# A slot's edges before the sums, the reciprocal behind the fold, and one stop at which nothing is evicted

## The chip, the cores and the metric

The kernel runs on one core of a Trainium2 chip. The metric is the device time of one execution in microseconds (us); lower is better. The engines are TensorE (PE in the profile, with its weight loads as PEld), VectorE (DVE), ScalarE (ACT), GpSimd (POOL) and SyncE (SP), which here only starts DMAs.

## The reference

Attention in which each query keeps its 32 highest scores, and then four matrix products on the result. All of it is float32.

```python
B, H, S, D = 8, 8, 576, 64
scores = (1.0 / np.sqrt(D)) * np.matmul(q, k.transpose(0, 1, 3, 2))
kth = np.partition(scores, -32, axis=-1)[..., -32:-31]
scores = np.where(scores >= kth, scores, -1000000000.0)
scores = scores - np.max(scores, axis=-1, keepdims=True)
attn = np.exp(scores)
attn = attn / (np.sum(attn, axis=-1, keepdims=True) + 1e-09)
x = np.matmul(attn, v).transpose(0, 2, 1, 3).reshape(B * S, H * D)   # 4608 x 512
return (((x @ w1) * (x @ w2)) @ w3) @ w_out                          # 512 -> 1024 -> 1024 -> 512
```

## The kernel before

The attention is cut into 144 **slots**, 18 for each of the 8 batches. A slot is 128 queries of two heads (the last 64 queries of two head pairs share a slot, the one with `t == 4`). The matrix products of a batch, 576 TensorE instructions, are handed out during the 18 slots of the next batch, 32 a slot. Those of the last batch come behind the last slot. In the first 15 slots or so the weights are still fetched and decoded, by `warm()`.

The loop of line 514 is a software pipeline. In its turn `p` it computes the scores of slot `p+1`, finds the 32 highest of slot `p`, masks and exponentiates slot `p-1` (`j`) and multiplies slot `p-2` (`m`) with the values. Each engine works through its own queue in the order in which the loop issues, since `InOrder` (line 39) keeps the program order; semaphores are added where data demand it. The names of a turn, in the order of the queues:

- **fold** (VectorE, `top32_steps`, line 234): four tensor_tensor instructions that write `w` out of the scores `s`. Three rounds of MAX8 and MATCH_REPLACE8 follow, and a last MAX8 over 576 columns, which completes `top`. Last comes `xt`, the scaled output (`store_x`).
- **edge** and `over` (GpSimd, `edges_of`, line 257): tiny instructions on `top`. ScalarE's first step of masking (`mask`, called **relu** here: `pab<-s,edge`) needs the edge. GpSimd's two subtractions `pab<-s,pab` follow, the first of them behind the next slot's fold, by a dependency written out by hand.
- **sums** (GpSimd) and **reciprocal** (VectorE), both in `invert`, line 295: 1e-9 is added to the two sums that ScalarE's second exponential has just completed, and they are inverted. TensorE spreads them over the partitions (`ro<-ident,sums`).
- **chunks' copy** (ScalarE, `take_turned`, line 313): the transposed weights `tp` go from PSUM to `pts`; TensorE's product with the values (`ro<-pts,vt`) waits for it.

The order at the top of a turn, lines 521 to 527:

```python
if 0 <= m < n_slots:
    invert(pabs[m][1])
folded = next(finder, None)
warm()
if 0 <= j < n_slots:
    edges[j] = edges_of(j)
    pabs[j] = new_weights()
```

The matrix products fill in at four stops of a turn, `fill(SHARE[0])` to `fill(SHARE[3])`, with 8, 3, 11 and 10 matmuls. What must be done when a PSUM tile is complete is **put off**: `moe_steps` appends it to `put_off`, and the next `fill` runs all of that list (`evict`, line 473) ahead of its matmuls. Put off are `asb` (ScalarE copies the product with w1), `whole` with its two followers `g` (VectorE multiplies it with the product with w2, ScalarE and GpSimd split the result into a high and a low part), `osb` (ScalarE copies the output) and `split_x` (`xf`, two ScalarE and two GpSimd instructions). Behind `fill(SHARE[1])` come TensorE's transposes `tp`, and ScalarE's chunks' copy. PSUM has three tiles for these products.

Of the kernel before, what the change touches and what calls it, by code (L numbers as in the profile page):

```python
# [34 lines left out]
SHARE = 8, 3, 11, 10  # L35
# [22 lines left out]
def attn_moe(ctx: ExitStack, tc: tile.TileContext, q, k, v, w1, w2, w3, w_out, out, flag, general):  # L58
# [123 lines left out]
    def new_ro():  # L182

        return ps_v.tile([128, 512], F32, tag="v", name="ro")

    def last_scores(pairs, t, ro):

        sc = ro[:, 384:]
        if t == 4:
            for a in range(2):  # L190
                qt, kt, _ = pairs[a]
                for i in range(2):
                    pe.matmul(
                        sc[:, a * 64 : a * 64 + 64], qt[:, MAIN:], kt[:, MAIN + i * 64 : MAIN + i * 64 + 64],
                        start=(i == 0), stop=(i == 1),
                    )
        else:
            qt, kt, _ = pairs[0]
            pe.matmul(sc, qt[:, t * 128 : (t + 1) * 128], kt[:, MAIN:], start=True, stop=True)
        return sc  # L200
# [19 lines left out]
    def new_s():  # L220
        return att_p.tile([128, 2, S], F32, tag="s", name="s", bufs=3)
# [5 lines left out]
    def take_last(s, sc):  # L227
        act.copy(flat(s)[:, MAIN : MAIN + 128], sc)

    def take_scores(s, st):  # L230
        to = s[:, :, :MAIN]
        act.copy(bass.AP(tensor=to.tensor, offset=to.offset, ap=[to.ap[0], [S + 64, 2], [1, MAIN]]), st)

    def top32_steps(s, slot):

        w = att_p.tile([128, 2, S], F32, tag="w", name="w", bufs=1)
        top = tops[slot % len(tops)]
        one, two, three = slice(0, NG), slice(NG, 2 * NG), slice(2 * NG, S)
        dve.tensor_tensor(w[:, :, three], s[:, :, one], s[:, :, two], op=ALU.max)
        dve.tensor_tensor(w[:, :, two], s[:, :, one], s[:, :, two], op=ALU.min)
        dve.tensor_tensor(w[:, :, one], w[:, :, three], s[:, :, three], op=ALU.max)
        yield dve.tensor_tensor(w[:, :, three], w[:, :, three], s[:, :, three], op=ALU.min)
        for i in range(4):
            cut = slice(i * 8, (i + 1) * 8)
            for a in range(2):  # L250
                dve.max(top[:, a, cut], w[:, a, one] if i < 3 else w[:, a, :])
            if i < 3:
                for a in range(2):
                    dve.match_replace(w[:, a, one], top[:, a, cut], w[:, a, one], NEG)
                yield

    def edges_of(slot):
        top = tops[slot % len(tops)]
        edge = small.tile([128, 2, 2], F32, tag="edge", name="edge")
        pool.tensor_tensor(edge, top[:, :, 0:32:31], coef, op=ALU.mult)  # L260
        pool.tensor_tensor(over[:, 2 * slot : 2 * slot + 2], top[:, :, 31], top[:, :, 23], op=ALU.subtract)
        return edge
# [15 lines left out]
    def new_weights():  # L278
        return att_p.tile([128, 2, S], F32, tag="pab", name="pab"), small.tile([128, 2], F32, tag="sums", name="sums")

    def mask(s, edge, pab, a, after=None):

        act.activation(pab[:, a, :], s[:, a, :], AF.Relu, bias=edge[:, a, 1:2], scale=-STEEP)
        ins = pool.tensor_tensor(pab[:, a, :], s[:, a, :], pab[:, a, :], op=ALU.subtract)
        if after is not None:
            tc.add_manual_dep(
                ins.ins, after.ins.name, mybir.DependencyInfo(mybir.DependencyClass.Sync, mybir.DependencyReason.DATA),
                reason="the fold of the next slot goes before the masking",
            )
# [5 lines left out]
    def invert(sums):  # L295
        pool.tensor_scalar(sums, sums, 1e-9, None, op0=ALU.add)
        dve.reciprocal(sums, sums)

    def turn(pab):

        tp = ps_a.tile([128, 2, 512], F32, tag="a", name="tp")
        for a in range(2):
            for c in range(4):
                n, o = (a * 4 + c) * 64, a * (S + 64) + c * 128
                for i, rows in enumerate(HEADS):
                    pe.transpose(tp[:, i, n : n + 64], flat(pab)[rows, o : o + 128], ident[rows, rows])
        return tp

    def turn_last(pab, ro):

        pe.transpose(ro[:, :128], flat(pab)[:, MAIN : MAIN + 128], ident)

    def take_turned(tp):
        pts = att_p.tile([128, 2, 512], F32, tag="pts", name="pts", bufs=1)
        act.copy(pts, tp)
        return pts

    def take_last_turned(ro):
        pr = att_p.tile([128, 128], F32, tag="pr", name="pr")
        act.copy(pr, ro[:, :128])  # L320
        return pr
# [146 lines left out]
    kv, ss, edges, pabs, xts = {}, {}, {}, {}, {}  # L468
# [4 lines left out]
    def evict():  # L473
        while put_off:
            put_off.pop(0)()

    def fill(n):
        evict()
        while queue and n:
            if next(queue[0], "end") == "end":  # L480
                queue.pop(0)
            else:
                n -= 1

    def pairs_of(i):
        return [kv[u] for u in slots[i][0]]

    def fetch_pair(u):
        if u < B * NHP:
            kv[u] = load_pair(u // NHP, u % NHP)  # L490
# [9 lines left out]
    def warm():  # L500

        if p < 0:
            return
        if fetched:
            z, step = fetched.pop(0)
            going.append(step(z))
        going[:] = [unit for unit in going if next(unit, "end") != "end"]
        prefetch(5)
# [4 lines left out]
    n_slots = len(slots)  # L513
    for p in range(-1, n_slots + 3):
        i, j, m = p + 1, p - 1, p - 2
        if i < n_slots and slots[i][1] == 3:
            fetch_pair(slots[i][0][0] + 2)
        while starting:
            queue.append(moe_steps(*starting.pop(0), put_off.append))
        finder = top32_steps(ss[p], p) if 0 <= p < n_slots else iter(())  # L520
        if 0 <= m < n_slots:
            invert(pabs[m][1])
        folded = next(finder, None)
        warm()
        if 0 <= j < n_slots:
            edges[j] = edges_of(j)
            pabs[j] = new_weights()
            for a in range(2):
                mask(ss[j], edges[j], pabs[j][0], a, folded if a == 0 else None)
        fill(SHARE[0])  # L530
        if 0 <= m < n_slots or i < n_slots:
            ro = new_ro()
        if 0 <= m < n_slots:
            turn_last(pabs[m][0], ro)
        if i < n_slots:
            sc = last_scores(pairs_of(i), slots[i][1], ro)
        if 0 <= m < n_slots:
            pr = take_last_turned(ro)
        if i < n_slots:
            ss[i] = new_s()  # L540
            take_last(ss[i], sc)
        fill(SHARE[1])
        next(finder, None)
        if 0 <= m < n_slots:
            tp = turn(pabs[m][0])
        if i < n_slots:
            st = scores(pairs_of(i), slots[i][1])
        if 0 <= m < n_slots:
            pts = take_turned(tp)
        if i < n_slots:  # L550
            take_scores(ss[i], st)
        warm()
        if 0 <= j < n_slots:
            exps(edges[j], *pabs[j], 0)
        if 0 <= m < n_slots:
            us, t = slots[m]
            for u in us:
                if u not in xts:
                    xts[u] = new_xt()
            ov, rb = values([kv[u][2] for u in us], t, pts, pr, pabs[m][1], ro)  # L560
            rec = take_rb(rb)
        if ready and (m + 1) % NS:
            put_off.append(lambda x=ready[0]: split_x(x[2], x[1], 0, 1))
            starting.append(ready.pop(0))
        fill(SHARE[2])
        next(finder, None)
        warm()
        if 0 <= j < n_slots:
            exps(edges[j], *pabs[j], 1)
        next(finder, None)  # L570
        warm()
        fill(SHARE[3])
        for _ in finder:
            pass
        if 0 <= m < n_slots:
            store_x([xts[u] for u in us], t, ov, rec)
            del ss[m], pabs[m], edges[m]
            if (m + 1) % NS == 0:
                ready.append((m // NS, [xts[m // NS * NHP + hp] for hp in range(NHP)], ([], [])))
                put_off.append(lambda x=ready[0]: split_x(x[2], x[1], 0, 0))  # L580
        warm()
# [69 lines left out]
```

## Time and profile before

| | |
|---|---|
| median of 3 runs | 1362.36 us (1360.36 to 1364.18) |
| profiled execution: its time, its span | 1362.26 us, 1360.5 us |
| PE, DVE, ACT, POOL busy | 1249.0, 1159.1, 980.7, 792.1 us |
| PEld busy | 1019.4 us |
| first and last relu start | 20.4, 1253.3 us |

The profiled execution is within 0.1 us of the median, and its span is 1.8 us shorter than its time. The span has three parts: the first 207 us, in which weights are prepared and VectorE hardly rests; from there to 1253 us slot after slot beside the matrix products; and the products that are left, to the end. The middle part repeats itself every 18 slots to within 0.03 us.

### The profile page before, as it was taken

To read this page: it belongs to the slowest core of one execution; us is meant where nothing else is said; L and a number is where in the kernel's file an instruction comes from. 1 tells how busy PE (TensorE), PEld (TensorE's weight loads), DVE (VectorE), ACT (ScalarE), POOL (GpSimd) and SP (SyncE) were. 2 spreads that over 40 slices of the span, in tenths; PEclk is the share of its full clock that TensorE was granted. 3 is DMA by queue.
4 is the path that set the end of the run, shared out by engine and by line. 5 is a ranking of instruction groups with operands and counts; after the bars stand their busy time and mean duration, and the time that the engine had idled before them with its cause. 6 is when DMAs were issued, how large, how long until landed. Compare 5 with 4: busy or idle time off the path is not lost.

```text
span 1360.5 us, 33364 instructions
## 1 busy us (share of the span) xinstructions
PE 1249.0 (92%) x12049; PEld 1019.4 (75%) x12049; DVE 1159.1 (85%) x4060; ACT 980.7 (72%) x2169; POOL 792.1 (58%) x1033
## 2 busy tenths in 40 slices
PE   3788846999999999999999999999999999999996
PEld 1444433788888888888888888888888888888996
DVE  7999999898989899999989898989999998987000
ACT  5777787777777777777777777777777777777221
POOL 3677696665656556565566565655656556656220
PEclk9998968999999999999999999999999999999998
DMA  6443431002020201011010202020101101000000
GB/s 221 117 132 104 137 93 31 21 17 64 13 68 12 68 13 52 29 44 36 25 44 17 64 12 68 13 68 12 49 32 45 36 14 56 16 15 2 19 18 21
DMA packets 34754, 65.15 MB, mean 48 GB/s; under 512 B 3860, under 2 KB 12052, under 8 KB 34580
## 3 DMA queue, kind: packets, MB, share of 16 engines
q1 hardware_dynamic: 34580, 62.93, 14.7%
q8 instruction: 97, 1.59, 0.5%
q14 instruction: 77, 0.63, 0.1%
HBM read 53.48 MB, written 9.44 MB: 46 GB/s over the span
## 4 chain that ended last, share of the span: by engine, by line
PE 54%; DVE 25%; ACT 8%; POOL 6%; issue 3%; DMA 1%; SPq 0%; DVEq 0%; POOLq 0%; ACTq 0%
PE ab L49 16%; PE eo L49 14%; PE ro L49 14%; DVE w L49 11%; DVE top L49 9%; PE st L49 5%; PE tp L49 3%; POOL edge L49 3%; ACT pab L49 3%; ACT pts L49 2%; DVE whole L49 2%; PE pf L49 2%; POOL g L49 2%; DVE y L49 1%; DVE z L49 1%
## 5 line engine op out<-in xcount | busy, mean ns | idle before, releaser
L49 POOL TENSOR_TENSOR pab<-s,pab 128x576 f32<-128x576 f32 x288 | 400.9, 1414 | 196.9 <-DVE w L49 101.2
L49 DVE MAX8 top<-w 128x8 f32<-128x192 f32 (+1 forms) x1152 | 466.7, 446 | 0.0
L49 PE MATMUL ab<-xf,wh 128*128 128x288 f32 x2048 | 432.8, 299 | 0.5 <-POOL xf L49 0.5
L49 PEld LDWEIGHTS ab<-xf,wh 128*128 128x128 f32 x2048 | 333.5, 188 | 10.5 <-issue 9.9
L49 ACT ACTIVATE pab<-s,edge 128x576 f32<-128x576 f32 x288 | 208.0, 769 | 159.5 <-POOL edge L49 159.5
L49 PE MATMUL ab<-xf,wl 128*128 128x288 f32 x1024 | 310.5, 303 | 0.0
L49 DVE MATCH_REPLACE8 w<-top,w 128x192 f32<-128x192 f32 x864 | 289.2, 342 | 0.0
L49 ACT ACTIVATE pab<-pab,edge 128x576 f32<-128x576 f32 x288 | 227.6, 790 | 0.8 <-POOL pab L49 0.7
L49 PE MATMUL eo<-g,wf 128*128 128x288 f32 x1536 | 228.1, 300 | 0.0
L49 PEld LDWEIGHTS eo<-g,wf 128*128 128x128 f32 x1536 | 208.6, 188 | 7.0 <-issue 7.0
L49 PEld LDWEIGHTS ab<-xf,wl 128*128 128x128 f32 x1024 | 192.2, 188 | 3.3 <-issue 2.4
L49 PE MATMUL ro<-pts,vt 128*64 128x128 f32 (+1 forms) x2560 | 163.4, 272 | 26.8 <-ACT pts L49 26.7
L49 POOL TENSOR_TENSOR g<-whole,g 128x288 fp32r<-128x288 f32 x128 | 103.1, 806 | 117.3 <-ACT g L49 117.3
L49 ACT COPY pts<-tp 128x1024 f32<-128x1024 f32 x144 | 146.0, 1014 | 32.7 <-PE tp L49 32.6
L49 PEld LDWEIGHTS ro<-pts,vt 128*64 128x64 f32 x2560 | 131.1, 140 | 48.9 <-ACT pts L49 42.3
L49 PE MATMUL st<-kt,qt 64*128 64x512 f32 (+1 forms) x640 | 165.7, 653 | 0.0
L49 DVE TENSOR_TENSOR w<-s 128x384 f32<-128x384 f32 x288 | 157.6, 587 | 8.7 <-ACT s L49 8.7
L49 DVE TENSOR_TENSOR w<-w,s 128x384 f32<-128x384 f32 x288 | 160.3, 557 | 4.9
L49 ACT COPY s<-st 128x1024 f32<-128x1024 f32 x144 | 147.0, 1021 | 4.0 <-PE st L49 3.9
L49 DVE TENSOR_TENSOR whole<-ab,asb 128x288 f32<-128x288 f32 x128 | 57.9, 452 | 99.1 <-PE ab L49 99.1
L49 PEld LDWEIGHTS ro<-ident,sums 128*64 128x64 f32 x640 | 31.0, 137 | 125.5 <-issue 50.8
L49 POOL TENSOR_SCALAR sums<-sums 128x2 f32<-128x2 f32 x144 | 30.7, 213 | 135.0 <-ACT pab L49 126.6
(52 smaller groups left out, 1572.6 us busy)
## 6 DMA issues: line engine op xcount, KB each, us to landing
z<-in_w SPq DMA_DIRECT2D x64, 256.0 KB, 2.6
vt<-in_v SPq DMA_DIRECT2D x32, 352.0 KB, 3.9
qt<-in_q SPq DMA_DIRECT2D x32, 320.0 KB, 3.0
kt<-in_k SPq DMA_DIRECT2D x32, 320.0 KB, 3.5
out_t<-osb SPq DMA_DIRECT2D x64, 144.0 KB, 1.8
z<-in_wo SPq DMA_DIRECT2D x16, 256.0 KB, 5.0
flag<-missed SPq DMA_DIRECT2D x1, 0.0 KB
seen<-flag SPq DMA_DIRECT2D x1, 0.0 KB
```

The costliest lines, as they stand in the source:

```text
L49: ins = fn(*args, **kw)
```

## The change

`edges_of` now stands ahead of `invert`, and `invert` behind the fold's issue and `warm()`. `fill` gets an argument `late`, with which it doesn't evict, and `fill(SHARE[1])` is called with it: what is put off in the first fill of a turn, or was going to be run at the second, is run at the third.

```diff
-    def fill(n):
-        evict()
+    def fill(n, late=False):
+        if not late:
+            evict()
         while queue and n:
...
         finder = top32_steps(ss[p], p) if 0 <= p < n_slots else iter(())
-        if 0 <= m < n_slots:
-            invert(pabs[m][1])
         folded = next(finder, None)
         warm()
         if 0 <= j < n_slots:
             edges[j] = edges_of(j)
+        if 0 <= m < n_slots:
+            invert(pabs[m][1])
+        if 0 <= j < n_slots:
             pabs[j] = new_weights()
...
-        fill(SHARE[1])
+        fill(SHARE[1], late=True)
         next(finder, None)
```

VectorE's queue in a turn whose first fill completes a product with w2 (`top_97` is one of three buffers that take turns), before:

```order
L49 TENSOR_TENSOR xt<-ro,rec 128x128
L49 RECIPROCAL sums<-sums 128x2
L49 TENSOR_TENSOR w<-s 128x2x192 x2
L49 TENSOR_TENSOR w<-w,s 128x2x192 x2
L49 TENSOR_TENSOR whole<-ab,asb 128x288
L49 MAX top_97<-w 128x8 x2
L49 MATCH_REPLACE w<-top_97,w 128x192 x2
```

and now:

```order
L49 TENSOR_TENSOR xt<-ro,rec 128x128
L49 TENSOR_TENSOR w<-s 128x2x192 x2
L49 TENSOR_TENSOR w<-w,s 128x2x192 x2
L49 RECIPROCAL sums<-sums 128x2
L49 MAX top_97<-w 128x8 x2
L49 MATCH_REPLACE w<-top_97,w 128x192 x2
L49 TENSOR_TENSOR whole<-ab,asb 128x288
```

The reciprocal moved from ahead of the fold to behind it, and `whole` from ahead of the first round to behind it.

GpSimd's queue in the same turn, before:

```order
L49 TENSOR_TENSOR g<-whole,g 128x288
L49 TENSOR_SCALAR sums<-sums 128x2
L49 TENSOR_TENSOR edge<-top_97,coef 128x4
L49 TENSOR_TENSOR over<-top_97 128x2
L49 TENSOR_TENSOR pab<-s,pab 128x576 x2
```

and now:

```order
L49 TENSOR_TENSOR g<-whole,g 128x288
L49 TENSOR_TENSOR edge<-top_97,coef 128x4
L49 TENSOR_TENSOR over<-top_97 128x2
L49 TENSOR_SCALAR sums<-sums 128x2
L49 TENSOR_TENSOR pab<-s,pab 128x576 x2
```

The edge and `over` passed the sums, and nothing else on GpSimd changed its place here.

ScalarE's queue in the same turn, before:

```order
L49 ACTIVATE pab<-s,edge 128x576 x2
L49 COPY asb<-ab 128x288
L49 COPY pr<-ro 128x128
L49 COPY s<-ro 128x128
L49 CAST g<-whole 128x288
L49 COPY pts<-tp 128x1024
L49 COPY s<-st 128x2x512
L49 ACTIVATE pab,sums<-pab,edge 128x576
L49 COPY rec<-ro 128x128
L49 ACTIVATE pab,sums<-pab,edge 128x576
```

and now:

```order
L49 ACTIVATE pab<-s,edge 128x576 x2
L49 COPY asb<-ab 128x288
L49 COPY pr<-ro 128x128
L49 COPY s<-ro 128x128
L49 COPY pts<-tp 128x1024
L49 COPY s<-st 128x2x512
L49 ACTIVATE pab,sums<-pab,edge 128x576
L49 COPY rec<-ro 128x128
L49 CAST g<-whole 128x288
L49 ACTIVATE pab,sums<-pab,edge 128x576
```

The cast `g` moved from ahead of the chunks' copy `pts` to behind `rec`. Over nine slots, which is half a batch, this move meets `whole` and `g` twice, `asb` twice, and `xf` and `osb` once each. TensorE's queue and SyncE's have the same order as before.

## Rows read from the trace of the kernel before

**Rows 1.** Stretches: us, busy PE, PEld, DVE, ACT, POOL (instructions); clock, DMA share, GB/s

```profile
0.00:207.00 207.00, 141.83 (x899) 74.89 (x899) 190.91 (x589) 151.44 (x369) 140.94 (x194) 0.90 0.44 132
555.17:702.90 147.73, 144.88 (x1492) 122.46 (x1492) 135.35 (x487) 113.62 (x246) 88.52 (x114) 1.00 0.12 37
```

**Rows 2.** Waits: engine, line <- releaser: us in total, times, longest us

```profile
ACT pab L49 <- POOL edge L49: 159.5, 142, 3.0
...
PE ro L49 <- ACT pts L49: 26.7, 68, 1.3
```

**Rows 3.** Timeline, TensorE, four slots: start, us, what [idle before <-releaser]

```profile
592.59 1.09 PE L49 MATMUL ro<-pts,vt 128*64 128x128 f32 x16 [0.84 <-ACT pts L49]
...
706.03 0.44 PE L49 MATMUL ro<-ident,sums 128*64 128x128 f32 x4
706.84 1.09 PE L49 MATMUL ro<-pts,vt 128*64 128x128 f32 x16 [0.36 <-ACT pts L49]
...
715.05 0.69 PE L49 MATMUL ro<-pts,vt 128*64 128x64 f32 x16 [0.16 <-ACT pts L49]
...
722.71 0.44 PE L49 MATMUL ro<-ident,sums 128*64 128x128 f32 x4
723.03 1.09 PE L49 MATMUL ro<-pts,vt 128*64 128x128 f32 x16
```

**Rows 4.** Timeline, ScalarE, the slots that start at 702.90 and 710.40 us

```profile
703.13 1.44 ACT L49 ACTIVATE pab<-s,edge 128x576 f32<-128x576 f32 x2 [1.49 <-POOL edge L49]
...
704.92 0.27 ACT L49 COPY s<-ro 128x128 f32<-128x128 f32 x1
705.44 0.43 ACT L49 CAST g<-whole 128x288 fp32r<-128x288 f32 x1 [0.24 <-DVE whole L49]
705.78 1.00 ACT L49 COPY pts<-tp 128x1024 f32<-128x1024 f32 x1
...
712.00 1.44 ACT L49 ACTIVATE pab<-s,edge 128x576 f32<-128x576 f32 x2 [2.02 <-POOL edge L49]
...
713.83 0.26 ACT L49 COPY s<-ro 128x128 f32<-128x128 f32 x1
713.98 1.02 ACT L49 COPY pts<-tp 128x1024 f32<-128x1024 f32 x1
```

**Rows 5.** Timeline, GpSimd, the same two slots

```profile
702.61 0.21 POOL L49 TENSOR_SCALAR sums<-sums 128x2 f32<-128x2 f32 x1
702.90 0.20 POOL L49 TENSOR_TENSOR edge<-top,coef 128x4 f32<-128x4 f32 x1
703.05 0.51 POOL L49 TENSOR_TENSOR over<-top 128x2 f32<-128x2 f32 x1
...
710.40 1.56 POOL L49 TENSOR_TENSOR edge<-top,coef 128x4 f32<-128x4 f32 x1 [0.72 <-DVE top L49]
```

**Rows 6.** Timeline, VectorE, the same two slots and the end of a third

```profile
702.42 0.27 DVE L49 TENSOR_TENSOR xt<-ro,rec 128x128 f32<-128x128 f32 x1
702.86 0.17 DVE L49 RECIPROCAL sums<-sums 128x2 f32<-128x2 f32 x1 [0.16 <-POOL sums L49]
702.94 1.04 DVE L49 TENSOR_TENSOR w<-s 128x384 f32<-128x384 f32 x2
703.90 1.14 DVE L49 TENSOR_TENSOR w<-w,s 128x384 f32<-128x384 f32 x2
...
710.17 0.27 DVE L49 TENSOR_TENSOR xt<-ro,rec 128x128 f32<-128x128 f32 x1
...
710.44 1.00 DVE L49 TENSOR_TENSOR w<-s 128x384 f32<-128x384 f32 x2
...
725.31 0.46 DVE L49 TENSOR_TENSOR whole<-ab,asb 128x288 f32<-128x288 f32 x1 [1.31 <-PE ab L49]
```

**Rows 7.** Timeline, VectorE's fold and a GpSimd addition in the first part

```profile
179.23 1.54 DVE L49 TENSOR_TENSOR w<-s 128x384 f32<-128x384 f32 x2
...
179.32 1.03 POOL L49 TENSOR_TENSOR y<-y 128x256 int32<-128x256 int32 x1 [0.46 <-DVE sums L49]
```

## The prediction, made before the result was known

> **What bounds the kernel now.** I read the stretches first. In 147.7 us, which are 18 slots in the middle of the span, TensorE is busy for 144.88 us at a clock of 1.00, and VectorE for 135.35 [rows 1]. So TensorE has the most work there, and only 2.84 us of each such stretch are idle. In the first 207 us it is VectorE, with 190.91 busy [rows 1], which begins only when the first scores are there. What is left behind the last slot is matmuls in a row, and the change doesn't touch it.
>
> Next come the waits. ScalarE waits 142 times for an edge, 159.5 us in all [rows 2], which looks like the prize. It isn't, since most of these waits lie beside a busy TensorE. The row that counts is TensorE's own wait for the chunks' copy, 26.7 us in 68 slots [rows 2]. The reader is to look at what leads there, in the timelines of two slots that follow each other.
>
> Slot A starts at 702.90. GpSimd adds to the sums, then makes the edge [rows 5]; relu starts at 703.13 and `pts` at 705.78, behind the cast `g`, which had waited for `whole` [rows 4]. TensorE's values start at 706.84 [rows 3]. Slot B follows: VectorE gives `top` at 710.26 (0.09 before that `xt` starts at 710.17 [rows 6]), the edge starts at 710.40 and takes 1.56 us in place of 0.20 [rows 5], relu starts at 712.00 [rows 4], and TensorE waits 0.16 [rows 3]. In the third slot, C, nothing is waited for on TensorE, while VectorE waits 1.31 us for a product at its end [rows 3, 6]. So A and B go by VectorE's chain, and C by TensorE, and what VectorE saves in A and B is not owed elsewhere.
>
> **What TensorE can get back.** In C the values start 0.32 us behind the spreading of the sums (722.71 to 723.03), in A 0.81 (706.03 to 706.84) [rows 3]. A therefore loses 0.49, of which the row shows 0.36, since modelled ends hide 0.13. Of the slots that run beside the products, 27 are like A, 9 have a wait like the 0.84 at 592.59 (there `xf` stands ahead of the copy; 0.97 lost), 14 are like B with 0.16, and 6 lie between (0.18 shown, 0.31 lost) (one slot of each of the first three stands in [rows 3]). Together 27 x 0.49 + 9 x 0.97 + 14 x 0.16 + 6 x 0.31 = 13.2 + 8.7 + 2.2 + 1.9 = 26.0 us. This is the most that the middle can give, as TensorE is full in every other slot.
>
> **The change part by part.** It adds and removes no instruction; TensorE's and SyncE's queues stay.
>
> *The late fill.* `pts` no longer stands behind `g`, `xf`, `asb` or `osb`. In A, relu's start to the copy `s` is 703.13 to 704.92, 1.79, and `s` to `pts` is 0.15 where nothing lies between (713.83 to 713.98) [rows 4]. So `pts` could start 1.94 behind relu; now it is 2.65. TensorE is ready for the values at 706.03 + 0.32 = 706.35, and they start 1.06 behind `pts` (705.78 to 706.84) [rows 3, 4]; `pts` must then start by 705.29 and relu by 703.35. Before, relu was at 703.13. By this part alone the wait in A goes. What is moved costs: `g`, `asb` or `xf` delays the second exponential by 0.3 to 0.8 us. Its reader is the sums' addition, which the edge no longer stands behind. `whole` comes one round later on VectorE. Its PSUM tile is wanted again three products later, and only three matmuls lie between the old stop and the new, so I cost that at nothing. If that cover were gone, TensorE would stand for the length of a round.
>
> *The reciprocal behind the fold.* In A it ends a wait: `xt` starts at 702.42, the reciprocal at 702.86, the fold at 702.94. In B nothing is waited for, and `xt` to fold is 0.27, of which 0.08 is the reciprocal's [rows 6]. So the fold in A starts 0.19 behind `xt`, at 702.61, 0.33 earlier; the reciprocal gives 0.08 back behind the fold. VectorE is 0.25 earlier in B. What is queued behind the reciprocal now is the first round, and if the sums come late it stands. They come behind the edge and `over`, which I follow next.
>
> *The edge ahead of the sums.* In A it could start 0.29 earlier by the queue (702.61 [rows 5]), but not before `top`. In B it started 0.23 behind `xt` [rows 5, 6], so in A at 702.65. That is 0.04 **behind** the fold's new start, and the same holds in almost every slot. Before, the reciprocal kept the fold just behind the edge. Here lies the uncertain term, as GpSimd's instructions stretch when they meet the fold: `over`, 0.11 behind the fold's start, took 0.51 and ended at 703.56, as the fold's first instruction ended; an addition 0.09 behind such a start took 1.03, and it was the fold that waited then (1.54 for two, against 1.04) [rows 5 to 7]. But the edge in B, 0.04 *ahead* of the fold, took 1.56, to the end of its third instruction. Bounds for the edge are thus 0.20 and 1.56, and the whole fold, 2.10 us (702.94 to 705.04 [rows 6]), cannot be excluded. I take 0.55: the new start lies behind the fold's, as in the two rows that waited for one instruction, and not ahead of it.
>
> The Trainium skill, "SBUF — State Buffer", "Who interferes with whom", says that a VectorE instruction with two SBUF inputs and a GpSimd instruction that reads SBUF exclude each other for a whole instruction, whichever started first. It speaks against the new order, in which the edge always comes second; by it an edge waits for one fold instruction, which is the 0.55. The `over` in A agrees (0.51), the edge in B (1.56) doesn't.
>
> With 0.55 relu in A starts at 702.65 + 0.55 + 0.04 = 703.24 (the 0.04 is 712.00 behind 711.96 [rows 4, 5]). That is 0.11 inside the 703.35: the wait of 0.49 goes. In B `top` comes 0.25 earlier, the edge at 710.15, relu at 710.74. TensorE, 0.49 earlier, would want `pts` at 715.05 - 0.16 - 0.49 - 1.06 = 713.34, so relu at 711.36, 1.98 before it [rows 3, 4]. That holds with 0.6 to spare, and the other 15 slots have `xf` or more out of the way too. `over` then passes in the gap behind the second fold instruction, and the sums behind the third, about 1.6 us after the fold's start; the fold ends at 2.1, so the reciprocal doesn't wait.
>
> *The first 207 us and the end.* VectorE is full there, no reciprocal waits, and the moves change its order alone: nothing, plus or minus 2 us.
>
> **The sum.** 26.0 us, less 1 for slots of A's kind in which 0.11 isn't enough: 25. Against the execution's 1362.3 us, which is the median too, that gives 1337 us. Its own range is 1333 to 1343.
>
> **The rivals.**
>
> *A-slots gain, B-slots don't.* In B the edge is held to the third instruction as now, in A not. Relu in B is then at 710.11 + 1.52 + 0.04 = 711.67 and `pts` at 713.65, 0.31 late for the 713.34. The sum is 13.2 - 14 x (0.31 - 0.16) + 9 x (0.97 - 0.31) + 6 x (0.31 - 0.31) = 17.0 us: 1345. For it: both kinds exist side by side now. Against: the starts are alike in A and B after the change.
>
> *Every edge is held to the third instruction.* Relu in A: 702.61 + 1.52 + 0.04 = 704.17, `pts` 706.11, 0.82 late in place of 0.49. That loses 0.33 x 27 = 8.9. TensorE is then so late that all waits of the other 29 slots go (12.8). 4 us are gained: 1358, at the edge of what a measurement of this kernel can tell from no change (0.3%, 4.1 us). For it: 28 edges like B's, all released by `top`, as the new ones are. The late fill would be eaten by the edges.
>
> *Every edge waits out the fold* (slower). Edges at 702.61 + 2.10 give relu at 704.75, `pts` at 706.69, 1.40 late: 0.91 x 27 = 24.6 lost against 12.8 gained, and the sums, last on GpSimd, then hold the reciprocal by half a microsecond in each slot, which uses up VectorE's reserve of 1.31 in three slots. 1374. It decides from an edge of 1.66 us on: there 27 times the extra loss is the 12.8. For it: nothing lies between B's 1.56 and this but 0.1 us. Against: behind the third instruction B's edge always got through.
>
> **How the numbers follow.** 0.52 for the forecast, 0.13 for the second case, 0.21 for the third (of it 0.05 beyond the 0.3%), 0.14 for the slower one. Faster by over 0.3%: 0.52 + 0.13 + 0.05 = 0.70; within: 0.16; slower: 0.14. The range takes in the first three, 1333 to 1362.
>
> **What would show it.** Right: TensorE's wait for `pts` is down from 26.7 us to under 8 (the first and last slots keep theirs), edges of about 0.5 us, folds that start 0.19 behind `xt`, and 18 slots in about 144 us. Wrong: edges of 1.5 us in all slots, with the wait on `pts` still there; or the reciprocal idle behind the fold. A wait of TensorE for a PSUM tile that `whole` or `asb` has not read would overturn the late fill.

## The result, and the profile after

The changed kernel takes 1345.76 us (median of 4 runs, 1344.96 to 1346.03) against 1362.36 us: 0.9878 of the time before, with a 95% interval of 0.9861 to 0.9895. That is 16.6 us less. 25 us had been forecast, 1337 us with its own range of 1333 to 1343; the time lies outside that and inside the range stated in the end, 1333 to 1362, which takes in two of the rivals. It is the time that the first rival gave, "A-slots gain, B-slots don't", 1345 us.

The stretches of after, with the columns of [rows 1]. The second line is again 18 slots, from one edge of kind A to the one 18 slots later:

```profile
0.00:207.00 207.00, 142.74 (x909) 76.28 (x911) 191.21 (x597) 152.88 (x371) 147.00 (x195) 0.90 0.43 134
548.79:694.48 145.69, 144.41 (x1492) 122.45 (x1491) 136.78 (x488) 111.95 (x246) 101.10 (x114) 1.00 0.11 38
```

Eighteen slots take 145.69 us in place of 147.73 [rows 1], 2.04 less. TensorE's idle time there is 1.28 in place of 2.85; the other 0.47 is in the busy time of the same 1492 matmuls, whose ends are modelled. From the 21st slot's transposes to the last slot's it is 994.78 us in place of 1010.31: 15.5 of the 16.6 us, of which 1.0 is what the first of these stretches gains beyond the others. The 21st slot's transposes start at 250.29 in place of 251.37, which is the other 1.1.

The waits of after, beside [rows 2] (us in total, times, longest):

```profile
ACT pab L49 <- POOL edge L49: 220.4, 134, 2.9
...
PE ro L49 <- ACT pts L49: 13.6, 38, 0.8
```

and GpSimd's edges, with their mean of 1035 ns (busy us, mean ns, then the idle time before them):

```profile
L49 POOL TENSOR_TENSOR edge<-top,coef 128x4 f32<-128x4 f32 x144 | 149.0, 1035 | 127.0 <-DVE top L49 123.4
```

TensorE's wait for the chunks' copy is halved, from 26.7 us to 13.6, not down to under 8. ScalarE's wait for edges has *grown* from 159.5 us to 220.4, and the kernel is faster all the same: most of that wait is covered by TensorE's work, as it was before.

What became of the slots A and B is in the timelines. VectorE (slot A starts with the `xt` at 694.25, B with that at 701.71):

```profile
694.25 0.27 DVE L49 TENSOR_TENSOR xt<-ro,rec 128x128 f32<-128x128 f32 x1
694.44 1.02 DVE L49 TENSOR_TENSOR w<-s 128x384 f32<-128x384 f32 x2
695.38 1.14 DVE L49 TENSOR_TENSOR w<-w,s 128x384 f32<-128x384 f32 x2
696.44 0.16 DVE L49 RECIPROCAL sums<-sums 128x2 f32<-128x2 f32 x1
...
701.71 0.27 DVE L49 TENSOR_TENSOR xt<-ro,rec 128x128 f32<-128x128 f32 x1
701.90 1.02 DVE L49 TENSOR_TENSOR w<-s 128x384 f32<-128x384 f32 x2
```

GpSimd, the same slots:

```profile
694.48 0.57 POOL L49 TENSOR_TENSOR edge<-top,coef 128x4 f32<-128x4 f32 x1
...
701.94 1.51 POOL L49 TENSOR_TENSOR edge<-top,coef 128x4 f32<-128x4 f32 x1 [0.77 <-DVE top L49]
```

ScalarE:

```profile
695.08 1.44 ACT L49 ACTIVATE pab<-s,edge 128x576 f32<-128x576 f32 x2 [1.60 <-POOL edge L49]
...
696.86 0.27 ACT L49 COPY s<-ro 128x128 f32<-128x128 f32 x1
697.11 1.01 ACT L49 COPY pts<-tp 128x1024 f32<-128x1024 f32 x1
...
703.48 1.44 ACT L49 ACTIVATE pab<-s,edge 128x576 f32<-128x576 f32 x2 [2.10 <-POOL edge L49]
704.83 0.42 ACT L49 CAST g<-whole 128x288 fp32r<-128x288 f32 x1
...
705.47 1.02 ACT L49 COPY pts<-tp 128x1024 f32<-128x1024 f32 x1
```

TensorE:

```profile
697.86 0.44 PE L49 MATMUL ro<-ident,sums 128*64 128x128 f32 x4
698.18 1.09 PE L49 MATMUL ro<-pts,vt 128*64 128x128 f32 x16
...
705.77 0.46 PE L49 MATMUL ro<-ident,sums 128*64 128x64 f32 x8
706.54 0.69 PE L49 MATMUL ro<-pts,vt 128*64 128x64 f32 x16 [0.31 <-ACT pts L49]
```

The fold starts 0.19 behind `xt` in both slots and the reciprocal waits for nothing. The edge starts 0.04 behind the fold in both. In A it takes 0.57 us, one fold instruction, and in B 1.51, three of them. Between relu and `pts` nothing is left in A but the copies (`asb`, `pr`, `s`), and the values follow the sums' spreading by 0.32, as in C [rows 3]. In B the late relu leaves TensorE a wait of 0.31, where it was 0.16.

The edges of the trace from the 21st slot on: 28 of 0.56 or 0.57 (all in A's place, behind a `g`), 74 of 1.50 to 1.57 (B, C and the rest; 14 of them are recorded 0.02 to 0.03 ahead of the fold, the others 0.03 to 0.05 behind it), 14 of 0.51 or 0.52 (queued behind `xf`, well after the fold's start), 8 of 0.20.

A useful measure for what follows is the time from one slot's transposes (`ro<-ident,pab`) to the next one's, all read from TensorE's timeline. It was 8.41 us for A and is 7.91. For B with `t == 4` it was 8.29 and is 8.43; for the B-slot with `xf` ahead of the copy 8.88 and 8.36; for the other B 8.22 and 8.36. All the other slots are as they were, to within 0.05.

### The profile page after: what moved, and what is told of

It is laid out like the page before. It is cut to its first block, busy times and chain, and to the rows that moved or that the text cites. A ratio compares the mean times of both kernels' runs of the same rounds, so it can differ in the third digit from the quotient of the medians.

```text
span 1343.9 us, 33367 instructions
## 1 busy us (share of the span) xinstructions
PE 1247.5 (93%) x12049; PEld 1020.8 (76%) x12049; DVE 1168.9 (87%) x4060; ACT 968.6 (72%) x2169; POOL 885.2 (66%) x1033
## 4 chain that ended last, share of the span: by engine, by line
PE 52%; DVE 31%; ACT 7%; issue 4%; POOL 4%; DMA 0%; DVEq 0%; POOLq 0%; SPq 0%; ACTq 0%
PE ab L49 17%; PE eo L49 14%; PE ro L49 13%; DVE top L49 12%; DVE w L49 11%; PE st L49 5%; POOL edge L49 3%; PE tp L49 3%; ACT pab L49 3%; ACT pts L49 2%; DVE y L49 2%; DVE z L49 2%; DVE whole L49 2%; DVE xt L49 1%; ACT pr L49 1%
## 5 line engine op out<-in xcount | busy, mean ns | idle before, releaser
L49 ACT ACTIVATE pab<-s,edge 128x576 f32<-128x576 f32 x288 | 207.9, 770 | 220.4 <-POOL edge L49 220.4
L49 POOL TENSOR_TENSOR edge<-top,coef 128x4 f32<-128x4 f32 x144 | 149.0, 1035 | 127.0 <-DVE top L49 123.4
L49 PE MATMUL ro<-pts,vt 128*64 128x128 f32 (+1 forms) x2560 | 164.8, 273 | 13.7 <-ACT pts L49 13.6
L49 DVE TENSOR_TENSOR w<-w,s 128x384 f32<-128x384 f32 x288 | 168.3, 584 | 4.9
L49 DVE TENSOR_TENSOR w<-s 128x384 f32<-128x384 f32 x288 | 160.6, 599 | 8.5 <-ACT s L49 8.5
## 6 DMA issues: line engine op xcount, KB each, us to landing
z<-in_w SPq DMA_DIRECT2D x64, 256.0 KB, 2.6
z<-in_wo SPq DMA_DIRECT2D x16, 256.0 KB, 5.1
```

Of the source, the lines that this page charges most:

```text
L49: ins = fn(*args, **kw)
```

## Experiments

Times are medians. The ratio is to the kernel before, run on the same chip, with its 95% interval.

### The two halves of the change, each alone

The new order without the late fill (against after):

```diff
-        fill(SHARE[1], late=True)
+        fill(SHARE[1])
```

> The new order of edge, sums and reciprocal, with every eviction where it stood before. Theory (the chunks' copy waits for relu, and relu for an edge that collides with the fold): in A-slots the edge takes 0.57 us, relu is at 703.2, but the copy stands behind the cast g again, about 0.16 us late, so 0.33 of 0.49 us is gained in 27 slots; B-slots stay as they are. About 1353 us. Rival (the order is worth nothing, all 16.6 us come from the late fill): 1362 us.

Measured: 1362.42 us, ratio 1.0006 (0.9997 to 1.0016): nothing, the rival's number. A-slots 8.46 us, 18 slots 147.88. VectorE, GpSimd and ScalarE in an A-slot:

```profile
703.15 0.46 DVE L49 TENSOR_TENSOR whole<-ab,asb 128x288 f32<-128x288 f32 x1 [0.24 <-ACT asb L49]
```

```profile
700.79 0.56 POOL L49 TENSOR_TENSOR edge<-top,coef 128x4 f32<-128x4 f32 x1
```

```profile
701.39 1.44 ACT L49 ACTIVATE pab<-s,edge 128x576 f32<-128x576 f32 x2 [1.60 <-POOL edge L49]
702.74 0.38 ACT L49 COPY asb<-ab 128x288 f32<-128x288 f32 x1
...
703.65 0.43 ACT L49 CAST g<-whole 128x288 fp32r<-128x288 f32 x1 [0.19 <-DVE whole L49]
703.98 1.01 ACT L49 COPY pts<-tp 128x1024 f32<-128x1024 f32 x1
```

These rows read backwards as a chain: `pts` behind `g`, `g` behind `whole`, `whole` behind `asb`, `asb` behind relu, relu behind the edge. VectorE's fold is 0.33 earlier, and then `whole` waits 0.24 for `asb`. On this chain the edge's 0.56 takes away what the reciprocal gave: relu starts 0.82 behind `xt`, where it was 0.71, and from relu to `pts` it is 2.59, against 2.65 before. An earlier fold alone buys nothing, because the chain goes over ScalarE.

The late fill without the new order (against before):

```diff
-    def fill(n):
-        evict()
+    def fill(n, late=False):
+        if not late:
+            evict()
...
-        fill(SHARE[1])
+        fill(SHARE[1], late=True)
```

> The late fill alone, with the old order of sums, edge and reciprocal. Theory: TensorE's wait of 0.49 us in 27 A-slots goes (13.2 us), but VectorE is not earlier, so the B-slots behind them wait 0.49 us longer (14 and 6 of them, -9.8 us) and the nine with xf gain 0.17 each (1.5 us): about 1357 us. Rival (the late fill is the whole of it): 1346 us. Rival (the parts add up to 16.6 with e1): together with e1 the gains make 16 us.

Measured: 1356.53 us, ratio 0.9965 (0.9951 to 0.9979), as expected. A-slots fall to 7.91 us, their whole loss, and the next slot gives it back: B with `t == 4` rises from 8.29 to 8.78. The pair A and B takes 16.69 us, and took 16.70 before. VectorE's queue through the two slots sets that sum, and this half leaves it alone. Only the pair with `xf` gains (8.41 + 8.88 before, 7.91 + 8.71 now).

So the halves are worth 0 and about 5 us alone and 16.6 together: the late fill takes `g` and its like out of the chain from relu to `pts`, and the order shortens VectorE's way through the pair. Which part of the order does it wasn't run alone: there is no kernel with the reciprocal behind the fold and the sums still ahead of the edge.

### Away with the edge's wait in B

If the edges of 1.5 us hold back the other 8 us, a kernel in which VectorE makes the edge itself, between `xt` and the fold, must get them:

```diff
-        pool.tensor_tensor(edge, top[:, :, 0:32:31], coef, op=ALU.mult)
+        dve.tensor_tensor(edge, top[:, :, 0:32:31], coef, op=ALU.mult)
...
-        folded = next(finder, None)
-        warm()
         if 0 <= j < n_slots:
             edges[j] = edges_of(j)
+        folded = next(finder, None)
+        warm()
```

> The changed kernel with the edge made by VectorE between xt and the fold, in place of GpSimd; over stays on GpSimd. Theory (what is left of TensorE's wait for the chunks' copy, about 11 us in 29 slots, is the edge held by the fold for three instructions, 1.51 us): relu starts about 0.35 us behind top in every slot, the wait goes, 1334 to 1337 us, though VectorE has about 0.1 us more in each slot. Rival (the B-slots are late because VectorE itself is full through A and B): no gain or a loss by the added 0.1 us a slot, 1345 to 1350 us.

Measured: 1344.32 us, ratio 0.9863 (0.9839 to 0.9888). The steady part does what was expected: 18 slots in 144.97 us, and TensorE waits 5.5 us for `pts`. The total doesn't, as the 21st slot's transposes start at 256.0, 5.7 us later than in after. This was one of the two long executions (1346.44 and 1347.53 us); the other two took 1340.56 and 1342.2, and whether they lost the same time at the start isn't known. Two stretches there, of the profiled one (the seventh number is the granted clock):

```profile
235.00:240.00 5.00, 5.00 (x37) 3.27 (x39) 4.97 (x22) 4.60 (x9) 4.31 (x4) 0.50 0.01 3
...
245.00:250.00 5.00, 5.00 (x34) 3.00 (x33) 4.41 (x21) 1.45 (x3) 3.26 (x5) 0.50 0.00 0
```

and the same of after:

```profile
235.00:240.00 5.00, 4.30 (x35) 2.39 (x35) 4.96 (x22) 5.00 (x13) 4.31 (x6) 0.86 0.01 3
...
245.00:250.00 5.00, 4.92 (x47) 4.75 (x48) 5.00 (x18) 2.91 (x8) 2.70 (x2) 1.00 0.40 134
```

In both stretches TensorE has the lower of its two levels, 0.50 of full speed (1.2 GHz), and is busy throughout. In the 20 us ahead of them TensorE was busy for 12.19 us at a clock of 0.84, and in after for 13.62 at 0.76. Why it fell there and not in after isn't settled. To see whether it is the start alone, the edge went to VectorE only from the 21st slot on:

```diff
+        if 20 <= j < n_slots:
+            edges[j] = edges_of(j, dve)
...
-        if 0 <= j < n_slots:
+        if 0 <= j < min(20, n_slots):
             edges[j] = edges_of(j)
```

> The edge on VectorE from slot 20 on, on GpSimd in the changed kernel's order before. Theory (e3 reached 144.96 us for 18 slots, 0.73 less than the changed kernel, and lost 5.7 us before slot 20, where TensorE's granted clock stood at 0.50 for 10 us): the start is as in the changed kernel, the steady part as in e3, 1340 to 1342 us. Rival (e3's loss belongs to VectorE's edges beside the products as well): 1344 us as e3.

Measured: 1342.34 us, ratio 0.9855 (0.9838 to 0.9871), with the 21st slot's transposes at 250.89: the start is within 0.6 us of that of after. The steady part isn't that of the kernel with all edges on VectorE. The profiled execution, 1345.26 us and the longest of its four, takes 144.9 to 145.9 us for 18 slots, though the code there is the same, and why is open. The time lies between the two numbers that were expected, and its interval overlaps that of the other kernel, so it doesn't decide between them.

### One edge per head

```diff
-        pool.tensor_tensor(edge, top[:, :, 0:32:31], coef, op=ALU.mult)
+        for a in range(2):
+            pool.tensor_tensor(edge[:, a, :], top[:, a, 0:32:31], coef[:, a, :], op=ALU.mult)
```

> The changed kernel with an edge for each head: that of the first head can start 0.66 us before top is complete, far ahead of the fold. Theory: the first relu starts before top is complete or as soon as ScalarE is free, only the second head's edge meets the fold (0.6 to 1.5 us); the two relus end some 0.67 us earlier in B-slots, which wait 0.31 to 0.33: that wait goes, 1335 to 1340 us. Rival (one more instruction in the fight for the fold's gaps delays the second edge by another fold instruction): B-slots gain nothing, 1345 to 1350 us.

Measured: 1344.93 us, ratio 0.9884 (0.9861 to 0.9907), not the 1335 to 1340 that was expected but nearly the rival's 1345. The first head's edge is now free of the fold, the second head's takes the whole loss, in slot B:

```profile
556.29 0.19 POOL L49 TENSOR_TENSOR edge<-top,coef 128x2 f32<-128x2 f32 x1
556.89 1.56 POOL L49 TENSOR_TENSOR edge<-top,coef 128x2 f32<-128x2 f32 x1 [0.41 <-DVE top L49]
```

Half an edge waits as long as a whole one: it is not the size of GpSimd's work that stretches, but the time until it gets through. The 18 slots fall to 145.22 us, B with `t == 4` gains 0.11, and the later start (252.15 for the 21st slot) takes more than half of that back.

### What decides between one fold instruction and three

In A GpSimd comes to its edge straight from `g`, which ends 0.13 before; in B and C it has been idle for at least 0.55. A theory was that an idle GpSimd has to wait for three instructions. Three clearings, released by the first head's last maxima, keep it busy up to the edge:

```diff
+            ins = pool.memset(spare, 0.0)
+            tc.add_manual_dep(
...
+            pool.memset(spare, 0.0)
+            pool.memset(spare, 0.0)
             edges[j] = edges_of(j)
```

> The changed kernel with three memsets of 128x160 on GpSimd ahead of each edge, released by the last MAX8 of the first head, so that GpSimd works until just before the edge, as it does in A-slots, where g ends 0.13 us before it. Theory (an edge that starts on a GpSimd that has been idle is passed over twice, one behind other work only once): B-slots' edges fall from 1.51 to about 0.57 us, TensorE's wait for the copy goes, 1336 to 1341 us. Rival (what VectorE does before the fold decides, or the slot's kind): edges of 1.51 us stay where they are, 1345 us or more.

Measured: 1356.9 us, ratio 0.9964 (0.995 to 0.9978). GpSimd in A, in B and in a slot of another kind, where the folds start at 551.58, 559.24 and 606.70:

```profile
551.43 0.81 POOL L49 MEMSET spare<- 128x160 f32 x3
552.21 0.45 POOL L49 TENSOR_TENSOR edge<-top,coef 128x4 f32<-128x4 f32 x1
...
558.66 0.81 POOL L49 MEMSET spare<- 128x160 f32 x3
559.44 1.35 POOL L49 TENSOR_TENSOR edge<-top,coef 128x4 f32<-128x4 f32 x1
...
606.71 0.60 POOL L49 TENSOR_TENSOR edge<-top,coef 128x4 f32<-128x4 f32 x1
```

The theory fell as it stands: a busy GpSimd isn't enough. In B the edge follows the last clearing without a pause, 0.20 behind the fold's start, and still ends with the fold's third instruction, 1.55 behind it. In A it comes 0.63 behind the fold's start and ends 1.08 behind it, with the instruction that was running. But the clearings also made the edges later: where three instructions passed, the edge starts 0.07 to 0.21 behind the fold (once 0.44). In seven slots it still starts 0.01 to 0.03 behind, and there it takes 0.58 to 0.60, one instruction; in after the same kind of slot had a GpSimd idle for 2.1 us and an edge of 1.50 or 1.51, 0.04 behind.

So idle time is not ruled out, and the other traces speak for it. From the 21st slot on, the edges of before start 0.02 to 0.04 ahead of the fold: 95 on a GpSimd that has been idle for 0.09 at most take 0.20, and 28 after 0.72 or more take 1.56 (one of each is in [rows 5]). In after all 28 edges with at most 0.14 of idle time ahead of them are passed by one instruction, and all 74 with 0.55 or more by three. The two halves of the change alone split in the same way, without an exception. Close to the fold's start the idle time thus goes with the outcome in four traces; whether it causes it, and why a busy GpSimd that comes 0.07 later is passed by three as well, is open.

### A gap ahead of the fold

If the edge has only to be through before the fold starts, a delay of the fold should do it. VectorE clears a tile of 128x128 that nobody reads, between `xt` and the fold:

```diff
+        dve.memset(gap, 0.0)
         folded = next(finder, None)
```

> The changed kernel with a memset of 128x128 on VectorE that does nothing, between xt and the fold, so that the fold starts about 0.1 us later and the edge on GpSimd stands ahead of it. Theory (a collision with the fold's start): edges take 0.20 us in place of 0.57 and 1.51, TensorE's wait goes, 1335 to 1339 us in spite of the added work. Rival (VectorE is what is late): 0.1 us more in each slot, 1346 to 1352 us; edges of 1.5 us stay if the start of the fold has nothing to do with it.

Measured: **1339.98 us, ratio 0.9836 (0.982 to 0.9853)**, faster than both kernels. Eighteen slots take 144.96 us, and TensorE's wait for `pts` is 5.0 us in all. VectorE and GpSimd in A, B and C:

```profile
547.98 0.17 DVE L49 MEMSET gap<- 128x128 f32 x1
548.06 0.96 DVE L49 TENSOR_TENSOR w<-s 128x384 f32<-128x384 f32 x2
...
563.14 0.17 DVE L49 MEMSET gap<- 128x128 f32 x1
563.22 0.96 DVE L49 TENSOR_TENSOR w<-s 128x384 f32<-128x384 f32 x2
```

```profile
547.96 0.65 POOL L49 TENSOR_TENSOR edge<-top,coef 128x4 f32<-128x4 f32 x1
...
555.50 0.65 POOL L49 TENSOR_TENSOR edge<-top,coef 128x4 f32<-128x4 f32 x1 [0.83 <-DVE top L49]
...
563.05 0.20 POOL L49 TENSOR_TENSOR edge<-top,coef 128x4 f32<-128x4 f32 x1 [1.71 <-DVE top L49]
```

An edge 0.10 ahead of the fold still loses one instruction, but one only, and in B too, so the expected 0.20 came in few slots; 0.17 ahead the edge takes its bare 0.20. The recorded distance alone is no rule: with the new order alone, without a clearing, six edges 0.08 to 0.09 ahead took 0.20. With a clearing VectorE has more to do and the kernel is faster.

The clearing from the 21st slot on alone, and two of them there:

```diff
+        if p >= 20:
+            dve.memset(gap, 0.0)
         folded = next(finder, None)
```

> After, with one clearing of a 128x128 tile on VectorE between xt and the fold, from slot 20 on alone (e5_gap had it in every slot). Theory (the gain of e5_gap lies in the slots beside the products, and its clearings in the first 150 us, where VectorE is full, cost 20 x 0.165 = 3.3 us): 18 slots as in e5_gap, 144.96, and the start as in after: 1337 to 1339. Rival (VectorE at the start isn't what sets the end, the gain stays as it was): 1340, as e5_gap.

> As e9_gap_late, with two such clearings, so that the edge starts some 0.27 ahead of the fold. Theory (the recorded distance of edge and fold decides: 0.04 to 0.10 ahead or behind meets the fold, 0.14 and more ahead is free): edges of 0.20 us in all slots, relu 0.45 earlier than with one clearing, 18 slots 144.9 to 145.2 (TensorE is nearly full already), 1337 to 1340. Rival (an edge near a fold is always held by at least one instruction, since the gap is still short): edges of 0.6 to 1.5 us, relu not earlier, and the second clearing costs VectorE 0.165 a slot: 1339 to 1343.

Measured: one clearing 1340.22 us, ratio 0.9846 (0.9828 to 0.9864), which is the time of the kernel with one in every slot, so the clearings at the start cost nothing that can be measured: the rival's number. Two clearings: 1354.21 us, ratio 0.9947 (0.9931 to 0.9964). There the theory on the distance was right (110 of 124 edges start 0.36 or more ahead and take 0.20, the other 14 stand behind `xf`; relu follows 0.23 behind the edge's start) and its time was wrong by 14 us; the rival's was wrong too. The B-slot with `t == 4`, first with one clearing, VectorE, then ScalarE:

```profile
556.35 0.43 DVE L49 TENSOR_TENSOR whole<-ab,asb 128x288 f32<-128x288 f32 x1
```

```profile
554.91 1.45 ACT L49 ACTIVATE pab<-s,edge 128x576 f32<-128x576 f32 x2 [1.32 <-POOL edge L49]
556.81 0.43 ACT L49 CAST g<-whole 128x288 fp32r<-128x288 f32 x1 [0.46 <-DVE whole L49]
...
557.47 1.02 ACT L49 COPY pts<-tp 128x1024 f32<-128x1024 f32 x1
```

and with two:

```profile
561.32 0.44 DVE L49 TENSOR_TENSOR whole<-ab,asb 128x288 f32<-128x288 f32 x1
```

```profile
559.17 1.44 ACT L49 ACTIVATE pab<-s,edge 128x576 f32<-128x576 f32 x2 [1.14 <-POOL edge L49]
561.79 0.43 ACT L49 CAST g<-whole 128x288 fp32r<-128x288 f32 x1 [1.17 <-DVE whole L49]
...
562.44 1.02 ACT L49 COPY pts<-tp 128x1024 f32<-128x1024 f32 x1
```

```profile
563.51 0.69 PE L49 MATMUL ro<-pts,vt 128*64 128x64 f32 x16 [0.46 <-ACT pts L49]
```

In B, `whole` and `g` were put off in the turn before, and are run at the first stop, ahead of the copy: the late fill doesn't touch them. As soon as relu is early, `g` waits for `whole` (0.46 us with one clearing, 1.17 with two), and B goes by VectorE's fold and `whole` instead. The second clearing delays those by 0.25 in A and 0.25 in B (`xt` to fold is 0.58 in place of 0.33), and the pair takes 16.65 us in place of 16.13, 0.52 more; with four such pairs 18 slots take about 147.0 us in place of 144.9 to 145.0. This is the next bound: with the edges out of the way VectorE's queue sets the pair.

### All of GpSimd's small work ahead of the fold

The reciprocal back ahead of the fold, behind the edge and the sums (against after):

```diff
-        folded = next(finder, None)
-        warm()
         if 0 <= j < n_slots:
             edges[j] = edges_of(j)
         if 0 <= m < n_slots:
             invert(pabs[m][1])
+        folded = next(finder, None)
+        warm()
```

> The changed kernel with edge, over, sums and reciprocal all ahead of the fold: the edge before the sums and the late fill stay, the reciprocal goes back. Theory (the fold's early start is worth more than the clean edge): edges take 0.20 us, but the fold waits for edge, over and sums on GpSimd, some 0.7 us behind xt in each slot in place of 0.19; VectorE is then full, about 24.9 us in three slots against 24.3 of the changed kernel, 1355 to 1375 us. Rival (the edge's 1.51 us is what costs): 1338 to 1345 us.

Measured: 1384.91 us, ratio 1.0171 (1.0154 to 1.0188), slower than before, and 10 us beyond what was expected. Every edge takes 0.20, and VectorE waits for the sums instead:

```profile
554.28 0.27 DVE L49 TENSOR_TENSOR xt<-ro,rec 128x128 f32<-128x128 f32 x1
555.19 0.17 DVE L49 RECIPROCAL sums<-sums 128x2 f32<-128x2 f32 x1 [0.63 <-POOL sums L49]
555.27 1.01 DVE L49 TENSOR_TENSOR w<-s 128x384 f32<-128x384 f32 x2
```

The fold starts 0.99 behind `xt`, in place of 0.19. A takes 7.91 us and B 9.43 to 9.51: the pair A and B is 17.4 us, where it was 16.70 before the change. So with the sums last on GpSimd, the change can't do without the reciprocal's place behind the fold.

## Why the prediction was right, and where it fell short

**The direction and the path: right; the number: by the width of the range.** The kernel got faster where and by the wait that the prediction named. That the time lies inside 1333 to 1362 is owed to the range, which reaches from the forecast to no gain at all. The case that came, edges held in B and not in A, had been given 0.13.

**What bounds the kernel: right.** 15.5 of the 16.6 us lie where the wait for `pts` was, in the slots beside the products. The start gave 1.1 us, inside its plus or minus 2.

**The late fill: right.** A's relu at 695.08 is 1.78 ahead of the copy `s`, as predicted, and the wait of 0.49 is gone: 8.41 to 7.91 us. No wait of TensorE shows a cost of the copies that are moved, and `whole` one round later made it wait for no PSUM tile.

**The reciprocal: right.** The fold starts 0.19 behind `xt` in most slots, and the reciprocal stood in nine only (VectorE's wait for the sums is down from 44.7 us to 5.1). The kernel with everything ahead of the fold shows what its place is worth in the new order of GpSimd, 39 us (1384.91 against 1345.76).

**The edge: this is the term that was mis-sized.** Its bounds were 0.20 and 1.56, and 0.55 was taken for all slots because the new start lies behind the fold's. In A that is what it took, 0.57. In B, at the same recorded 0.04 behind, it took 1.51. The text had the row against it: B's edge of 1.56 in before, 0.04 ahead of the fold [rows 5]. That row was set aside by the sign of a distance of 0.04 us. The sign meant nothing: in after 14 edges 0.02 to 0.03 ahead take 1.57, and in the kernel with the gap an edge 0.10 ahead waits for one instruction. A row of the same instruction in the same slot was better evidence than rows of other instructions at a like distance. The second rival had the better sign in hand: the 28 long edges of before were "all released by `top`, as the new ones are", on a GpSimd that had been idle. "The starts are alike in A and B", put against the first rival, held for the distance to the fold alone; in A the edge followed `g` after 0.13 us, in B it came after 0.77 of idle time. With 1.52 in B the prediction's own rival gave 17.0 us, and 16.6 came.

The rule of the Trainium skill, "SBUF — State Buffer", "Who interferes with whom", that the loser waits for one whole instruction, stood beside the 0.55. A agrees with it (0.57). The edges beside the clearing (0.65) were held by one instruction too, but were recorded ahead of the fold, and by that rule the one that starts first gets through. It doesn't describe the 74 edges of 1.50 to 1.57, which were passed over by three instructions in a row.

**The wait under 8 us: missed for that reason.** With the edge out of B's way, by the gap, it falls to 5.0, and 18 slots take 144.96; the prediction had under 8 and about 144. So the rest of the sum was nearly right, at 22 us of the 25.

**B's 0.6 to spare: wrong, and hidden.** The prediction took `pts` in B to follow relu by 1.98, and overlooked that `g`, which still stands between them in B (it is gone from there in A alone), waits for `whole` when relu comes early. With one clearing `pts` starts at 557.47, 3.47 behind the `xt` of its slot, and the clearing moves the fold by 0.14 (0.33 behind `xt` in place of 0.19): 3.33 without it, as an estimate. From the forecast's `xt`, 710.17 less 0.25, that is 713.25, against the 713.34 at which TensorE would want it. There was 0.09 us to spare, and the kernel with two clearings shows what happens beyond that.

**The rivals.** "A-slots gain, B-slots don't" came, with its number. "Every edge is held to the third instruction" was true of 74 edges in 124, and failed in A, where it decides the time. Of "every edge waits out the fold" nothing was seen: no edge that started beside the fold's first instruction went beyond its third.

## What to carry to other kernels

- Two queues that meet in pairs of slots have to be read as a pair. What the late fill saved in A came back in B to 0.01 us until VectorE's own queue was shorter too.
- A small instruction that another engine waits for should be clear of a row of large ones on its rival engine, not just ahead of it in the order: 0.17 us of room made 0.20 out of 1.57 in C, and a clearing that does nothing paid for itself. Twice that room cost more than it gave, since VectorE was the next bound.
- When a row of the trace is carried over to a new order, compare also what the engine did just before. The short edges of before followed the sums; the new order took the sums away, and most edges then came on an idle GpSimd, like the long ones.
- When a wait is removed from a chain, walk the queue between its two ends again and ask of each instruction what *it* waits for; here it was `g`, for `whole`.

## What was not expected of the hardware

GpSimd's edge, 0.20 us alone, was passed over by three VectorE instructions that followed each other, 74 times, and by one only 28 times, though both kinds started within 0.05 us of the first of them. It got in at the latest in the gap between the third and the fourth. In these 102 slots, and in those of three more kernels at the same distance, the edges on a GpSimd that had been idle for 0.2 us or more were the ones that waited for three. With GpSimd kept busy by clearings the edge waited for one when it came 0.01 to 0.03 behind the fold, and for three when it came 0.07 or more behind, within the fold's first instruction. What the mechanism is was not found.
